# v of two batches by casting transfers, bias rows pair by pair, and a new order of early transfers in an attention and mixer kernel on one Trainium2 core

## The chip, the cores and the metric

The kernel runs on one core of a Trainium2 chip. A core has engines with instruction queues of their own: PE (TensorE, matmuls and transposes), DVE (VectorE), ACT (ScalarE), POOL (GpSimd) and SP (SyncE, which here only issues transfers). Transfers that SP issues are on one hardware queue (q1), those of ACT on another (q10), those of POOL on a software queue (q0); all of them run on the same 16 DMA engines. Only transfers issued by POOL change a type on the way. The metric is the device time of one execution in microseconds, less is better. "The span" is the time from the first to the last instruction in one profiled execution.

## The reference

For 8 batches, 8 heads, 576 positions and a head width of 64, attention with a causal mask and a bias of running sums, and then a mixer:

```python
scores = scale * np.matmul(q, k.transpose(0, 1, 3, 2))
cum = np.cumsum(np.maximum(s, 0.0), axis=-1)
bias = -(cum[:, :, :, None] - cum[:, :, None, :])
scores = np.where(causal, -1000000000.0, scores + np.minimum(bias, 0.0))
attn = softmax(scores)
x = np.matmul(attn, v)              # heads side by side: 8 x 576 x 512
h = x.transpose(0, 2, 1) @ U @ V    # U: 576 x 32, V: 32 x 576
u = x + h.transpose(0, 2, 1)
out = u + np.maximum(u @ w_ch1, 0.0) @ w_ch2   # 512 x 2048, 2048 x 512
```

All inputs and the output are float32. `softmax` stands for the lines of the reference that subtract the maximum, take exp and divide by the sum.

## The kernel before, in words

**Stages.** Batches are taken in groups of two. For a batch, each head has `scores` (L290): matmuls of transposed keys with transposed queries in four PSUM banks, four exps on ACT into a buffer `p`, and one mask by POOL (`affine_select`, L317). `weigh` (L334) multiplies `p` with `v_raw`, whose rows have a 65th column of ones, so that the sums come along; DVE divides into `x_sb`. For a group, `mix` (L449; `mix_first` for batch 0) adds the low-rank part and transposes into `uT`, `layer1` makes `hT` with w1 and ReLU, `layer2` makes the output with w2.

**Bias.** It is part of the matmul: under the 64 rows of a head's keys and queries lie four more (`AUG`), with ones against the running sums, which are split in three bf16 parts. Keys and queries of a pair of heads are one slot of `kT` and `qT`, a ring of 8 slots; slots 0 to 3 are `kA[0]`, `qA[0]` (batch 0) and 4 to 7 `kA[1]`, `qA[1]` (batch 1). `direct_rows` (L239) sends the parts of batches 0 and 1 from `parts` straight into the slots. For batches 2 to 7 `keep_rows` (L246) stores them in DRAM (`aug`) and `bias_rows` (L257) loads four rows of a pair for the keys and four for the queries.

**Keys and queries.** Batches 0 and 1: `load_six` (L158) loads them as bf16 by POOL, PE transposes them (`turn_six`, L265) and DVE or ACT copies them into the slots. Batches 2 to 7: `cast(b)` (L149) is two transfers by POOL from k and q to bf16 in DRAM (`kq`); `turn_kq` (L165) is two transposing transfers by SP from there into a slot. `turn_batch(b)` (L708) issues `turn_kq` for the four pairs of a batch, each followed by the bias rows of the pair before.

**v.** `fetch_v(b, t)` (L184) loads a tile of 128 rows (the last of 64) as float32 by SP, 256 bytes a row and head, into `vf` (batch 1: into the memory of w2, `vf1`). `cast_v` (L190) turns it into bf16 in `v_raw` on POOL or DVE.

**Order.** The schedule is written out by hand, and each engine works in program order. The start (from L560) loads, clears and sums for batch 0. `first_attention` (L626) has the eight heads of batch 0, with `fill` matmuls between that give no result, then its eight weighs among `mix_first`. Batch 1 is `second_scores`, a generator with `second_at_head(h)` (L715) called after each head; `beside(back, ahead, ratio, lead)` (L545) steps two generators in turn by their costs, with `ahead` held back for `lead` units. L756 puts `layer1` of batch 0 beside batch 1's heads, weighs and mix. From L793 on, the two layers of a group stand beside the attention of the next one; `attention` calls `at_head(h)` (L773) after each head, which issues the transposes, casts and v of later batches. The first mask buffers `first_p` are eight, some lent from `x_sb[1]` and `v_flat[1]`.

Of the kernel before, what the change touches and what calls it, by code (L numbers as in the profile page):

```python
# [40 lines left out]
def kernel(  # L41
# [61 lines left out]
    def clear(ap, value=0.0, engine=None):  # L103
# [9 lines left out]
    vf1 = w2[:, :10, :].bitcast(FP32).rearrange(  # L113
        "p (t a) (b d) -> p t (a b) d", a=2, d=D
    )
# [65 lines left out]
    def staged(b):  # L181
        return vf1 if b == 1 else vf0

    def fetch_v(b, t):  # L184
        rows = slice(128 * t, min(128 * t + 128, S))
        nc.sync.dma_start(
            out=staged(b)[v_rows(t), t], in_=v[b, :, rows].rearrange("h p d -> p h d")
        )

    def cast_v(b, t, engine=None):  # L190
        n = v_rows(t)
        (engine or nc.gpsimd).tensor_copy(v_raw[b // 2 % 2][n, 5 * (b % 2) + t, :, :D], staged(b)[n, t])  # L192
# [46 lines left out]
    def direct_rows(b, p0, p1, r, queue=None):  # L239
        to = qA[b][D : D + 1] if r == 0 else kA[b][D + r : D + r + 1]  # L240
        (queue or nc.sync).dma_start(
            out=to[:, p0:p1, : 2 * S].rearrange("r n (j c) -> r n j c", c=CW),
            in_=parts[2 * SEG * p0 : 2 * SEG * p1, r, b, :],
        )
# [335 lines left out]
    )  # L580
    make_identity(nc, identity)
    load_six(0, 0, 2, 4)
# [28 lines left out]
    direct_rows(0, 0, HP - 1, 1)  # L611
    direct_rows(0, 0, HP - 1, 0, nc.scalar)
    next(sums)
    direct_rows(0, 0, HP - 1, 2)
    next(sums)
    direct_rows(0, 0, HP - 1, 3, nc.scalar)
    for t in (4, 0, 1, 2, 3):
        fetch_v(0, t)
    for r in range(AUG):
        direct_rows(0, HP - 1, HP, r)  # L620
    load_UV(0)
    for n in range(HP, RING):
        clear(qT[n][D:KA, : 2 * S], 1.0, nc.gpsimd)
    later = cumulate(2, B, nc.gpsimd)

    def first_attention():  # L626
# [11 lines left out]
        turns = [(2, 0, "f"), (2, 1, "pv"), (3, 0, "pv"), (3, 1, "f")]  # L638
        done = []
        for h in range(H):  # L640
            p = next_p()
            for _ in scores(h // 2, h % 2, p, fills=320 if 1 < h < 6 else 0):
                pass
            if turns:
                hp, which, tag = turns.pop(0)
                turn_six(0, hp, which, tag=tag)
            done.append((0, h, p))
            if h == 0:
                nc.vector.memset(v_raw[0][:, :, :, D : D + 1], 1.0)
                nc.sync.dma_start(  # L650
                    out=kA[1][D : D + 1].rearrange("r n (h s) -> r (n h) s", h=2),
                    in_=ones[:H],
                )
                for r in range(AUG):
                    direct_rows(1, 0, HP, r)
                load_UV(1)
                nc.sync.dma_start(out=kq[:, :, PAIR:].rearrange("i n c -> (i n) c"), in_=zeros)
                nc.sync.dma_start(
                    out=aug[1:4].rearrange("r n s -> n r s"),
                    in_=ones.unsqueeze(1).to_broadcast([BH, 3, S]),  # L660
                )
                for t in (4, 0, 1, 2, 3):
                    fetch_v(1, t)
            if h == 5:
                for t in range(5):
                    fetch_v(2, t)
            if h == 1:
                clear(U_cat[:, :, :], 0.0, nc.gpsimd)
            if h in (2, 3):
                load_six(1, 0, 4 * h - 8, 4 * h - 4)  # L670
                load_six(1, 1, 4 * h - 8, 4 * h - 4)
            if h == 3:
                load_w1(0)
                clear(V_cat[:, :, :], 0.0, nc.gpsimd)
            if h == 4:
                for t in (4, 0, 1, 2, 3):
                    cast_v(0, t, nc.vector)
                nc.vector.memset(v_raw[0][:64, TAIL], 0.0)
                place_UV(0)
            if h == 5:  # L680
                load_w1(1)
        for j in (2, 3):
            load_w1(j)
        nc.gpsimd.memset(v_raw[0][:64, 5 + TAIL], 0.0)
        halves = [mix_first(dt) for dt in (0, 2)]
        for _ in range(2):
            weigh(*done.pop(0))
        turn_six(1, 0, 0, scalar=2, tag="f")
        for _ in range(2):
            weigh(*done.pop(0))  # L690
        turn_six(1, 0, 1, scalar=2, tag="f")
# [3 lines left out]
        next(second_front)  # L695
        next(second_front)
        weigh(*done.pop(0))
        next(halves[0])
        weigh(*done.pop(0))
# [3 lines left out]
        next(second_front)  # L703
        next(second_front)
# [10 lines left out]
    def second_at_head(h):  # L715
        if h == 2:
            cast(2)
        if h == 3:
            place_UV(1)
        if h == 5:  # L720
            for t in (4, 0, 1):
                cast_v(1, t)
            for n in range(2 * HP, 3 * HP):
                turn_kq(n)
        if h == 6:
            for t in (2, 3):
                cast_v(1, t, nc.vector)
            next(later)
        if h >= 6:
            load_w2(2 * h - 12)  # L730
            load_w2(2 * h - 11)
# [5 lines left out]
    def second():  # L737
        yield from second_front
        for head in second_done:
            weigh(*head)  # L740
            yield 0.48
            next(later, None)
        keep_rows(2, B)
        for n in range(2 * HP, 3 * HP):
            bias_rows(n)
# [11 lines left out]
    for t in range(5):  # L757
        fetch_v(3, t)
    turn_batch(3)

    def both_layers(g):
        if g == 0:
            yield from layer2(0, range(4))
            yield from layer1(((576, 864), (864, 1152)))
            yield from layer2(0, range(4, 9))
        else:
            yield from layer1(THIRDS)
            yield from layer2(g, range(9))

    def ahead_of(c):  # L770


        def at_head(h):  # L773
            if h == 0 and 2 < c < B - 1:
                turn_batch(c + 1)
            if h == 4 and c + 2 < B:
# [16 lines left out]
    for g in range(len(GROUPS)):  # L793
# [5 lines left out]
        n_back = 46.8 if g == 0 else 61.4  # L799
        lead = 14.0 if g == 0 else 0.0  # L800
# [31 lines left out]
```

## Time and profile before

| | |
|---|---|
| runs | 391.14, 389.36, 390.70 us; median 390.7 |
| profiled execution | 390.39 us, span 388.7 us |
| mean granted clock of TensorE | 0.996 |
| transfers | 48.56 MB, 117,991 records |
| q0 (POOL) | 13,824 records, 13.63 MB, 22.4% of 16 engines' span |
| q1 (SP) | 103,558 records, 34.27 MB, 44.1% |
| batch 0, head 0: first scores on PE | 11.01 us |
| batch 2, head 0 | 86.62 us |
| batch 3, head 0 | 109.14 us |

How to read it. A line of a time line has the start in us, the duration, the engine, the line of the kernel, the operation, what it writes and reads, how many were merged, and in brackets how long the engine had been idle before and what ended that. "SPq" and "POOLq" rows, and POOL rows with DMA in the name, are instructions that issue a transfer; their duration is that of the issue, the data land later. Tiles have the names of their memory, so p buffers that are lent show as `x_sb` or `v_raw`, and the sums of batches 2 to 7 as `v_raw`. In a table by stretches each row has the stretch, its length, then busy time and count for PE, PEld (loading of weights, beside PE), DVE, ACT, POOL, then the granted clock as a share of full speed, the busy share of the 16 DMA engines (over 1 where records of several queues overlap) and GB/s. The trace also has a record for every piece that a DMA engine moved, with queue, start, duration and size as written.

### The profile page before, as it was taken

Reading aid. Unit: us, or ns where it says so; the run is one execution under the profiler, and the core shown is the slowest. Engines: PE = TensorE matmul, PEld = TensorE weight load, DVE = VectorE, ACT = ScalarE, POOL = GpSimd, SP = SyncE. Lnnn points to the kernel's source line nnn. Section 1 sums busy time; section 2 is a strip of 40 time slices with the busy share of each in tenths; the row PEclk is TensorE's granted clock in tenths of the full one; section 3 lists DMA queues with packets and bytes.
Section 4 is the critical chain, followed back from the end, with each engine's and each line's share of the span. In section 5 each row is a group of like instructions: output and inputs, shape, how many; then the busy total and the mean of one; then the engine's idle time right before and its main releaser. Section 6 shows DMA issues by size and latency. Waiting matters only on the chain.

```text
span 388.7 us, 8287 instructions
## 1 busy us (share of the span) xinstructions
PE 370.3 (95%) x3277; PEld 228.6 (59%) x3300; DVE 142.1 (37%) x308; ACT 209.1 (54%) x488; POOL 105.4 (27%) x173
## 2 busy tenths in 40 slices
PE   7879898989999999999999999999999999999995
PEld 3567675547876546666655456666655455665442
DVE  7867785222224392212143571212143570000221
ACT  5876984109996207898842007898842005773000
POOL 8981695013544301333142001233120000000000
PEclk9989999999999999999999999999999999999999
DMA  7999999999999969999996417800011111000122
GB/s 109 173 210 214 191 196 169 195 155 207 180 192 232 191 132 254 187 179 147 174 185 170 93 74 133 155 2 2 2 49 38 53 69 41 0 2 27 65 71 81
DMA packets 117991, 48.56 MB, mean 125 GB/s; under 512 B 99576, under 2 KB 113088, under 8 KB 117952
## 3 DMA queue, kind: packets, MB, share of 16 engines
q1 hardware_dynamic: 103558, 34.27, 44.1%
q0 software_dynamic: 13824, 13.63, 22.4%
q8 instruction: 26, 0.43, 0.5%
q10 hardware_dynamic: 570, 0.12, 0.2%
q14 instruction: 13, 0.11, 0.1%
HBM read 37.52 MB, written 16.97 MB: 140 GB/s over the span
## 4 chain that ended last, share of the span: by engine, by line
PE 80%; ACT 5%; DVE 5%; DMA 4%; SPq 3%; issue 1%; ACTq 0%; POOL 0%; DVEq 0%
PE ps_f L509 30%; PE ps_f L524 27%; PE ps_s L296 10%; PE ps_pv L346 7%; DMA kT<-parts 2%; SPq L170 2%; ACT pT L302 2%; PE ps_f L451 2%; PE ps_pv L469 2%; PE ps_f L484 2%; DMA qT<-aug_rows 1%; DVE qT L282 1%; DVE x_sb L488 1%; ACT hT L516 1%; DVE v_raw L224 1%
## 5 line engine op out<-in xcount | busy, mean ns | idle before, releaser
L509 PE MATMUL ps_f<-uT,w 128*128 128x384 bf16 (+3 forms) x832 | 157.6, 313 | 0.2 <-ACT hT L516 0.2
L302 ACT ACTIVATE pT<-ps_s 128x448 bf16<-128x448 f32 x232 | 109.1, 520 | 69.3 <-PE ps_s L296 68.0
L524 PE MATMUL ps_f<-w,hT 128*128 128x512 bf16 x554 | 138.7, 379 | 1.3
L516 ACT ACTIVATE hT<-ps_f 128x384 bf16<-128x384 f32 (+2 forms) x208 | 99.4, 479 | 65.9 <-PE ps_f L509 64.5
L509 PEld LDWEIGHTS <-w 128*128 128x128 bf16 x832 | 72.7, 98 | 33.8 <-issue 0.7
L317 POOL TENSOR_SCALAR_AFFINE_SELECT pT<-pT 128x640 bf16<-128x640 bf16 x58 | 43.6, 752 | 168.2 <-ACT pT L302 168.1
L296 PE MATMUL ps_s<-qT,kT 68*128 68x128 bf16 (+9 forms) x576 | 81.4, 240 | 7.4 <-DMA kT<-parts 3.1
L524 PEld LDWEIGHTS <-hT 128*128 128x128 bf16 x576 | 53.2, 98 | 55.0 <-issue 2.2
L296 PEld LDWEIGHTS <-kT 68*128 68x128 bf16 (+1 forms) x576 | 46.6, 97 | 37.0 <-issue 6.9
L533 DVE TENSOR_TENSOR o<-x_sb,ps_f 128x512 f32<-128x512 bf16 x36 | 24.7, 686 | 95.0 <-PE ps_f L524 81.1
L352 DVE RECIPROCAL rec<-ps_pv 128x5 f32<-128x5 f32 x64 | 12.4, 194 | 126.2 <-PE ps_pv L346 126.0
L346 PEld LDWEIGHTS <-pT 128*128 128x128 bf16 x870 | 34.7, 99 | 8.9 <-ACT pT L302 1.5
L346 PE MATMUL ps_pv<-v_raw,pT 128*128 128x65 bf16 x870 | 37.6, 196 | 1.0 <-ACT pT L302 0.7
L358 DVE TENSOR_TENSOR x_sb<-ps_pv,rec 128x320 bf16<-128x320 f32 (+1 forms) x64 | 29.3, 458 | 2.3
L488 DVE TENSOR_TENSOR x_sb<-x_sb,ps_f 128x512 bf16<-128x512 bf16 x32 | 21.2, 685 | 5.7 <-PE ps_f L484 5.6
L192 POOL CAST v_raw<-vf 128x512 bf16<-128x512 f32 (+1 forms) x30 | 17.9, 612 | 0.4
L476 DVE COPY uT<-ps_pv 128x1024 bf16<-128x1024 bf16 (+2 forms) x18 | 11.1, 623 | 2.5 <-PE ps_pv L469 2.4
L469 PEld LDWEIGHTS <-x_sb 128*128 128x128 bf16 x128 | 8.6, 98 | 4.1 <-DVE x_sb L488 0.2
L484 PE MATMUL ps_f<-ux_sb,V_cat 128*128 128x512 bf16 x27 | 10.2, 379 | 0.6 <-DVE o L533 0.4
L469 PE MATMUL ps_pv<-identity,x_sb 128*128 128x128 bf16 x128 | 10.3, 219 | 0.1
L288 PE MATMUL ps_s<-uT 128*128 128x512 bf16 (+1 forms) x22 | 8.1, 445 | 1.8 <-DVE uT L105 1.6
L451 PE MATMUL ps_f<-x_sb,U_cat 128*128 128x512 bf16 x31 | 8.7, 379 | 0.7 <-DVE x_sb L363 0.7
(104 smaller groups left out, 160.2 us busy)
## 6 DMA issues: line engine op xcount, KB each, us to landing
out_dram<-o SPq DMA_DIRECT2D x32, 256.0 KB
vf<-in_v_dram SPq DMA_DIRECT2D x28, 256.0 KB
w<-in_moe_w_ch_dram POOLq DMA_DIRECT2D x8, 512.0 KB, 9.9
kq_rows<-in_k_dram POOLq DMA_DIRECT2D x6, 576.0 KB, 6.5
kq_rows<-in_q_dram POOLq DMA_DIRECT2D x6, 576.0 KB, 9.6
w<-in_v_dram SPq DMA_DIRECT2D x4, 256.0 KB
out_dram<-o SPq DMA_DIRECT2D x8, 128.0 KB
vf<-in_v_dram SPq DMA_DIRECT2D x7, 128.0 KB
```

Source lines behind the costliest of these rows:

```text
L296: nc.tensor.matmul(ps[:, col : col + w], lhsT=kt_[:rows, c + kc : c + kc + 128], rhs=qt_[:rows, c + qc : c + qc + w], start=True, stop=True,)
L302: nc.scalar.activation(p[:, at : at + w], ps[:, :w], EXP, scale=scale)
L317: nc.gpsimd.affine_select(out=diagonal, in_=diagonal, compare_op=ALU.is_ge, fill=0.0, base=0, pattern=[[0, 5], [1, 128]], channel_multipli ...
L346: nc.tensor.matmul(pv3[:, it, :], lhsT=p[:, at : at + 128], rhs=vr[:, 5 * bi + j, h, :], start=(j == 0), stop=(j == it),)
L358: nc.vector.tensor_mul(x[:, 5 * bi : 5 * bi + n, h * D : h * D + D], pv3[:, :n, :D], rec[:, :n].unsqueeze(2).to_broadcast([128, n, D]),)
L469: nc.tensor.transpose(pb[:, d, m, :], x[:, t, 128 * d : 128 * d + 128], identity)
L484: nc.tensor.matmul(hp_, lhsT=V_cat[:, t, :], rhs=ux_sb, start=True, stop=True,)
L488: nc.vector.tensor_add(x[:, t, :], x[:, t, :], hp_)
L509: nc.tensor.matmul(f1[:, :cw], lhsT=w1[:, kt, 128 * nf : 128 * nf + 128], rhs=uT[:, kt, c0:c1], start=(kt == 0), stop=(kt == 3),)
L516: nc.scalar.activation(hT[:, nf, c0:c1], f1[:, :cw], RELU)
L524: nc.tensor.matmul(f2, lhsT=hT[:, kt, 128 * t : 128 * t + 128], rhs=w2[:, kt, :], start=(kt == 0), stop=(kt == 15 and not more),)
L533: nc.vector.tensor_add(o, x_sb[g % 2][:, t, :], f2)
```

## The change

- v of batches 0 and 1 comes by `load_v`, a transfer by POOL that writes bf16 in place into `v_raw`; the float32 stage in w2's memory, ten fetches by SP and ten casts go.
- Batch 0's bias rows go pair by pair: pair 0 first, then pairs 1 and 2, then pair 3, on SP. `direct_rows` writes the same bytes with heads and pieces as one dimension.
- Clears move from POOL to DVE; the ones under batch 1's queries come by three transfers by SP from `ones` instead of four clears.
- `load_six` of batch 1 is issued before the heads of batch 0, behind `load_v(0)`. Two turns of batch 1 go into heads 6 and 7 of batch 0, with all copies on DVE.
- Heads 0 to 2 of batch 0 are weighed after the scores of heads 5 to 7; batch 1's first ten steps go between the other weighs (four steps before).
- w2 is loaded at heads 1 to 4 of batch 1 (6 and 7 before), ahead of the cast of batch 2, which moves from head 2 to 5. The sums of batches 2 to 7 start at head 3 and are stored at head 7; behind them SP fetches v of batch 2 and turns batch 2 with its rows pair by pair.
- The cast of batch 3 (the "third cast"), its v and its transposes move from before batch 2's attention to behind its head 1.
- The first tile of `layer2` of group 0 moves into the stage beside batch 1, and the ratios follow.

The diff, cut to its core:

```diff
@@ the start
-    make_identity(nc, identity)
     load_six(0, 0, 2, 4)
+    make_identity(nc, identity)
     load_six(0, 1, 2, 4)
+    nc.vector.memset(v_raw[0][:, :, :, D : D + 1], 1.0)
...
-    for p in first_p:
-        nc.gpsimd.memset(p[:, PAD:D4], 1.0)
-    clear(ones, 1.0, nc.gpsimd)
-    clear(zeros, 0.0, nc.gpsimd)
+    for t in (4, 0, 1, 2, 3):
+        load_v(0, t)
+    for hs in ((0, 4), (4, 8)):
+        for i in range(2):
+            load_six(1, i, *hs)
...
-    direct_rows(0, 0, HP - 1, 1)
-    direct_rows(0, 0, HP - 1, 0, nc.scalar)
+    direct_rows(0, 0, 1, 1)
+    direct_rows(0, 0, 1, 0, nc.scalar)
...
-    for t in (4, 0, 1, 2, 3):
-        fetch_v(0, t)
-    for r in range(AUG):
-        direct_rows(0, HP - 1, HP, r)
+    for p0, p1 in ((1, HP - 1), (HP - 1, HP)):
+        for r in (1, 2, 0, 3):
+            direct_rows(0, p0, p1, r)
     load_UV(0)
-    for n in range(HP, RING):
-        clear(qT[n][D:KA, : 2 * S], 1.0, nc.gpsimd)
@@ new
+    def load_v(b, t):
+        rows = slice(128 * t, min(128 * t + 128, S))
+        nc.gpsimd.dma_start(
+            out=v_raw[0][v_rows(t), 5 * b + t, :, :D],
+            in_=v[b, :, rows].rearrange("h p d -> p h d"),
+        )
@@ first_attention, before the heads
+        clear(ones, 1.0)
+        clear(zeros, 0.0)
+        for p in first_p:
+            nc.vector.memset(p[:, PAD:D4], 1.0)
+        for i in (0, 1):
+            nc.vector.memset(v_raw[0][:64, TAIL + 5 * i], 0.0)
...
+        turns = [
+            (0, 2, 0, "f"), (0, 2, 1, "pv"), (0, 3, 0, "pv"), (0, 3, 1, "f"),
+            None, None, (1, 0, 0, "f"), (1, 0, 1, "f"),
+        ]
@@ in the heads
+            for _ in scores(h // 2, h % 2, p, fills=320 if 1 < h < 5 else 0):
...
+            if h >= 5:
+                weigh(*done.pop(0))
+            if h == 4:
                 load_w1(0)
+                clear(U_cat[:, :, :])
+                clear(V_cat[:, :, :])
+        weigh(*done.pop(0))
+        place_UV(0)
+        for j in (1, 2, 3):
             load_w1(j)
@@ second_at_head
+        if h == 0:
+            for t in (4, 0, 1, 2, 3):
+                load_v(1, t)
         if h == 2:
+            place_UV(1)
+        if 1 <= h <= 4:
+            load_w2(h - 1)
+        if 3 <= h:
+            next(later)
+        if h == 5:
             cast(2)
+        if h == 7:
+            keep_rows(2, B)
+            for t in range(5):
+                fetch_v(2, t)
+            turn_batch(2)
@@ second
-        nc.gpsimd.tensor_copy(warm[:1, :1], qT[2 * HP + HP - 1 - RING][:1, :1])
-        cast(3)
-    beside(layer1(PARTS, by_block=True), second(), 15.2 / 14.9, 0.0)
-    for t in range(5):
-        fetch_v(3, t)
-    turn_batch(3)
+    def first_layer():
+        yield from layer1(PARTS, by_block=True)
+        yield from layer2(0, range(1))
+    beside(first_layer(), second(), 15.2 / 18.3, 0.0)
@@ at_head of the later batches
+            if h == 1 and c == 2:
+                nc.gpsimd.tensor_copy(warm[:1, :1], qT[2 * HP + HP - 1 - RING][:1, :1])
+                cast(3)
+                for t in range(5):
+                    fetch_v(3, t)
+                turn_batch(3)
@@ the last loop
-        n_back = 46.8 if g == 0 else 61.4
-        lead = 14.0 if g == 0 else 0.0
+        n_back = 43.4 if g == 0 else 61.4
+        lead = 10.0 if g == 0 else 0.0
```

More of the change, by code (lines that the diff above doesn't have):

```diff
@@ L680, in first_attention @@
-            if h == 5:
-                load_w1(1)
-        for j in (2, 3):
+            if turns[h]:
+                b, hp, which, tag = turns[h]
+                turn_six(b, hp, which, tag=tag)
+            if h >= 5:
+                weigh(*done.pop(0))
+            if h == 4:
+                load_w1(0)
+                clear(U_cat[:, :, :])
[3 more added lines that the diff above has]
+        for j in (1, 2, 3):
             load_w1(j)
-        nc.gpsimd.memset(v_raw[0][:64, 5 + TAIL], 0.0)
@@ L685, in first_attention, with more @@
         halves = [mix_first(dt) for dt in (0, 2)]
[L686 to L691, printed above, removed]
+        def more(n):
+            for _ in range(n):
+                next(second_front)
+        more(2)
+        weigh(*done.pop(0))
+        more(2)
+        weigh(*done.pop(0))
+        more(2)
+        next(halves[0])
         weigh(*done.pop(0))
@@ L694, in first_attention @@
         weigh(*done.pop(0))
[L695 to L699, printed above, removed]
+        more(2)
         for _ in halves[0]:
@@ L702, in first_attention @@
         next(halves[1])
-        next(second_front)
-        next(second_front)
+        more(2)
         for _ in halves[1]:
```

88 lines of the change are left out of this document (22 added, 66 removed).

## The prediction

> **What bounds the kernel now.** I read the busy shares first, then the table by stretches, then the time lines of PE, SP and POOL around each wait of PE.
>
> ```profile
> PE 370.3 (95%) x3277; PEld 228.6 (59%) x3300; DVE 142.1 (37%) x308; ACT 209.1 (54%) x488; POOL 105.4 (27%) x173
> 0.00:11.00 11.00, 7.16 (x40) 3.05 (x41) 8.29 (x23) 5.46 (x8) 9.40 (x30) 1.00 0.82 115
> 11.00:19.50 8.50, 7.91 (x83) 5.51 (x84) 6.63 (x10) 8.10 (x21) 7.94 (x13) 1.00 0.96 175
> 19.50:24.50 5.00, 2.75 (x22) 1.52 (x20) 3.43 (x6) 3.67 (x10) 3.96 (x8) 0.92 1.32 210
> 24.50:35.00 10.50, 10.04 (x177) 8.75 (x175) 7.03 (x21) 6.93 (x14) 5.35 (x8) 0.88 1.26 216
> 35.00:55.00 20.00, 17.84 (x217) 13.55 (x217) 16.10 (x28) 17.82 (x48) 12.70 (x20) 1.00 1.12 197
> 200.00:240.00 40.00, 39.66 (x289) 21.61 (x291) 18.60 (x35) 9.32 (x21) 5.63 (x9) 1.00 0.53 125
> ```
>
> PE carries the end: from 95 us on it is over 98% busy until the tail. What an edit can win lies before that: about 11 us in which PE waits, and what fills (no result) and a low clock take. The column before last is the DMA share: in the first 95 us it is near or above 1, so there the transfers are the second bound. The waits of PE, with what ended them, and batch 3, which has none:
>
> ```profile
> 11.01 0.74 PE L296 MATMUL ps_s<-qT,kT 128*128 128x64 bf16 x7 [1.29 <-DMA kT<-parts]
> 21.96 0.74 PE L296 MATMUL ps_s<-qT,kT 128*128 128x64 bf16 x7 [1.76 <-DMA kT<-parts]
> 86.62 0.36 PE L296 MATMUL ps_s<-qT,kT 68*128 68x64 bf16 x4 [1.00 <-DMA qT<-aug_rows]
> 109.14 0.36 PE L296 MATMUL ps_s<-qT,kT 68*128 68x64 bf16 x4
> ```
>
> Heads 0 and 6 of batch 0 and head 0 of batch 2 wait for bias rows. Why rows and transposes can be late is on SP and POOL:
>
> ```profile
> 80.30 0.83 POOL L151 DMA_DIRECT2D kq_rows<-in_k_dram  x1
> 97.43 1.40 SPq L170 DMA_TRANSPOSE qT<-kq_rows  x1
> 99.18 0.74 POOL L151 DMA_DIRECT2D kq_rows<-in_k_dram  x1
> 102.06 6.16 SPq L170 DMA_TRANSPOSE qT<-kq_rows  x1
> 108.28 0.47 SPq L261 DMA_DIRECT2D kT<-aug_rows  x1
> ```
>
> A transpose takes 1.4 us alone and 6.16 us under the cast of batch 4 (issued 99.18). The DMA records of the trace say why: while both queues have work, POOL's (q0) and SP's (q1) alternate one record at a time, 281 against 282 at 46 to 48 us and 824 against 830 at 124 to 130, one pair per engine in about 0.115 us. Alone, q1 moves a 256-byte record per engine in about 16.5 ns. A transpose and a v fetch are 72 and 64 such records per engine, a cast of k or q 32.
>
> **The change part by part**, against the profiled execution (span 388.7, time 390.39; the runs' median, 390.7, is 0.3 higher and within their spread).
>
> Start. Pair 0's bias rows go alone: 18 pieces instead of 54. Row 3 was issued by ACT at 6.29 and landed at 10.76; its records began 2.1 to 2.4 us after the issue and trickled to 10.4, alternating with the six loads. With a third of them I put the landing at 9.2. The queries are copied at 8.7 and the second transposes are limited by their load (8.85 now), so head 0 starts at 9.4 instead of 11.0: **-1.6** (bounds 0 and -2.3, by the copies). The identity moved behind one load costs the first transposes 0.2, hidden behind DVE's sums, which run to 5.8 and free the copy. Pairs 1 to 3 follow on SP at 0.75 each and land near 12 and 15, ahead of heads 2 and 6: the 1.3 us that ACT lost before head 6 go (**-1.3**).
>
> Weights early. Three weighs at 0.48 and two turns at 0.25 leave the PE-bound stretch after 24.7 for heads 5 to 7, where ACT is the bound (1.6 us a head): **-1.9**.
>
> v by casting transfers. Removed: five DVE casts (3.2 us), five more of batch 1 (3.7 on POOL and DVE), ten SP fetches. Added: ten POOL issues; those of 192, 384 and 512 rows took 0.64, 0.68 and 0.76, so about 0.95 for 1024, 4.6 us per batch, with four loads of batch 1 (2.7) behind them. The clears that leave POOL (3.3 us) make room, and head 0's mask runs at about 17 instead of 13.1, which only the first weigh reads. The DVE clears (1.7) fall into its 1.5 us gap before 12.56; DVE is then full until 19 and head 6 waits 0.4 for it. The price that the trace lacks is a cast of 256 bytes. Lower bound: the plain 256-byte record, 18 ns. The line through the cast records (79, 96 and 106 ns for 1536, 2048 and 2304 bytes read) gives 34. Upper: 34 + 13 = 47, since a plain 128-byte record doubles from 13 to 26 where it is crowded. A cast of 2048 adds 12 ns to the plain 84, so 18 + 12 = **30 ns**, which I take: it starts from the record of the same size. 288 of them: 8.6 us per batch behind the six loads (11.3), so v(0) lands at 20.4 and the first k of batch 1 at 22.3. Weigh 0 wants v at 18.2, and PE is about 0.5 ahead of ACT there: **+1.7** (0 to 6.5, by the bounds); the turns at heads 6 and 7 wait **+0.7**. Together -1.6 - 1.3 - 1.9 + 1.7 + 0.7 = **-2.4** by the time layer 1 begins.
>
> Batch 1. Its heads start sooner, but DVE has more: the later sums (0.69 + 6 x 0.43 = 3.3 us) sit at head 3 instead of 6, among turns of 1.6 a head. I take 0 (-1 to +1.5). On q0 the rest follows without a gap: batch 1's q and k from 19.9 (4 x 1.85, by the spacing of their records), w1 (4 x 3.1), v(1) 8.6, w2 (4 x 3.1) to 61, the cast of batch 2 (2 x 3.5) to 68, and 2 us for what SP alternates in: 70. Layer 2 needs w2 near 67; were it late, PE would stand that long.
>
> Batch 2. SP fetches v(2), then has four transposes (1.35 each) and pair 0's rows: landed near 79. Before, keep_rows and rows came last. PE gets there at 86.6 - 1.0 - 2.4 = **83.2**, so the 1.0 wait goes: **-1.0**. Layer 2's first tile ahead of it is only moved, and `lead` falls with it.
>
> Batch 3. Here I expect the loss. The cast of batch 3 was issued at 80.30, 6.3 us ahead of batch 2; now it waits behind head 1's mask, 4.7 us after batch 2's start (88.19 + 2.9 - 86.62): 87.9, its records from 89.4 (1.5 after issue, as at 81.84 now). POOL's wait for the last transpose (84.8) is over by then; if not, the masks queue behind it. SP, done with batch 2's rows near 84 (8 x 1.35 + 4 x 0.65 after 70.5), sends four outputs (1.8 as now) and v(3), whose records start near 89. The cast of batch 4 follows at head 4 (12.6 after batch 2's start, as now), so q0 holds 2 x 64 = 128 records without a gap. q1 must move v(3), 288, and four transposes, 288, before pair 0's rows. Alternating: 128 x 0.115 = 14.7, to 104.1; the other 448 at 16.5 ns, 7.4, to 111.5; rows 0.5: **112.0**. PE arrives at 83.2 + 22.5 (109.14 - 86.62) + 0.2 (the new ratio) = 105.9. Stall: **+6.1**, and +0.2 for the ratio. The next pairs need 3.5 us each and heads use 5.5, so this happens once.
>
> Clock. After the 1.76 us wait at 20 the granted clock was 0.74 and 0.58 in two stretches of 2.5 us: 1.7 us lost. The 6 us wait I give the same, less what ACT's pace hides: **+1.5** (0 to 1.7); the early dip may recur behind the wait for v and I leave it in.
>
> Sum: -2.4 - 1.0 + 6.1 + 0.2 + 1.5 = +4.4, so 390.4 + 4.4 = **394.8**. v at 25 to 36 ns instead of 30 moves 576 records by -2.9 to +3.5: 392 to 398 is the likeliest case's own range.
>
> A rule against this. The Trainium skill (DMA: Bandwidth & Descriptors, Queues, rings and completion order) says that an engine goes round its queues a packet at a time, typically 9 to 17 descriptors. By it SP's 72 records would wait some 4 to 8 turns and no transpose would starve, which is the first rival's case; the counts of one to one and the 6.16 us speak against it here.
>
> **Rivals.** (1) Batch 3's data come in time: SP's records get through the casts. Then from the cast's landing (about 14 after batch 2's start) three transposes at 1.4 and rows end near 19, under 22.7, and the result is 390.4 - 3.4 + 0.2 = 387.2. For: batch 3 has 7 us in hand now. Against: the alternation. (2) A cheap v, 20 ns: 5.8 us per batch, no wait for v, PE at batch 2 at 81 and q0 done 5 us sooner, v(3) half through before the cast; batch 3 then waits about 3: 390.4 - 5.8 + 0.2 + 3 + 1 = 389. (3) A dear v: above about 45 ns v(0) lands at 24.8 and the wait at weigh 0 is 6 instead of 1.7; both batches together push the cast of batch 2 by 8.6 to near 79, the last transpose past 93 and, through POOL's wait, the records of the cast of batch 3 from 89.4 to 95.5: batch 3 starts near 118, and the time is 390.4 + 9 + 1.5 = 401.
>
> **How the numbers follow.** Forecast 0.53, rival 1 0.17, rival 2 0.15, rival 3 0.13, nothing of this 0.02. Predicted 394.8. The range 387 to 398.5 takes in rivals 1 and 2 and leaves out the dear v and tails; the likeliest alone has 392 to 398. About 0.5% (2 us) is what a measurement can tell: slower 0.60 (most of the forecast, rival 3), same 0.20 (rival 2, the forecast's low end), faster 0.20 (rival 1, some of 2).
>
> **What would show it.** Right: head 0 at 9 to 10; a wait of PE near 18 to 20 on v_raw from in_v; v's cast records near 30 ns; no wait at batch 2; one of 4 to 8 us at batch 3's first head on kT or qT, with two transposes of 5 us or more just before, then a dip of the clock. Wrong: batch 3 without a wait (rival 1), or PE waiting for w2, or for v of batch 1.

## The result, and the profile after

The changed kernel took 395.76 us (median of four runs, 394.49 to 397.32), the kernel before 390.92 (389.36 to 393.07) beside it: ratio 1.0125, 95% interval 1.0088 to 1.0162, slower by 4.8 us. Where a median of the kernel before stands below, it is over all its runs on that chip; the ratios leave disturbed runs out.

The profiled execution of the changed kernel is the longest of the four: 397.32, span 395.6, against 388.7 before. First the busy shares, then the table by stretches:

```profile
PE 371.8 (94%) x3298; PEld 229.6 (58%) x3298; DVE 141.9 (36%) x318; ACT 206.2 (52%) x484; POOL 106.5 (27%) x163
```

```profile
11.00:19.50 8.50, 7.48 (x79) 5.10 (x80) 8.16 (x21) 7.76 (x20) 8.45 (x13) 1.00 2.14 146
19.50:24.50 5.00, 4.50 (x79) 3.37 (x77) 3.66 (x8) 4.87 (x14) 3.20 (x5) 1.00 1.35 206
24.50:35.00 10.50, 7.96 (x130) 6.80 (x127) 8.31 (x20) 3.84 (x10) 8.58 (x13) 0.84 1.18 202
75.00:95.00 20.00, 20.00 (x186) 12.87 (x184) 4.13 (x9) 10.27 (x28) 4.56 (x7) 1.00 0.77 174
95.00:115.00 20.00, 12.51 (x164) 9.94 (x161) 3.43 (x10) 11.35 (x31) 7.25 (x11) 0.84 1.18 184
115.00:135.00 20.00, 20.00 (x228) 13.93 (x226) 6.15 (x19) 15.31 (x37) 8.32 (x12) 0.90 1.03 188
```

PE's total is nearly the same. It is fuller than before from 19.5 to 24.5 and from 75 to 95, and emptier from 24.5 to 35 (7.96, it was 10.04). From 95 to 115 it is missing 7.5 us, and the clock stays down into the next stretch. The time line of PE has the waits:

```profile
11.06 0.74 PE L297 MATMUL ps_s<-qT,kT 128*128 128x64 bf16 x7 [1.02 <-DMA kT<-parts]
20.48 0.62 PE L347 MATMUL ps_pv<-v_raw,pT 128*128 128x65 bf16 x15
26.85 0.91 PE L297 MATMUL ps_s<-qT,kT 68*128 68x64 bf16 x6 [1.27 <-DMA w<-in_moe_U_dram]
84.16 0.55 PE L297 MATMUL ps_s<-qT,kT 68*128 68x64 bf16 x6
113.75 0.53 PE L297 MATMUL ps_s<-qT,kT 68*128 68x64 bf16 x4 [7.40 <-DMA qT<-aug_rows]
```

Head 0 still starts at 11; the wait ahead of head 6 is gone (head 6 at 20.94, it was 21.96); the first weigh (20.48) does not wait for v; batch 1's head 0 has a new wait (the bracket names a load of U, which these matmuls do not read; experiments 9 and 10 show what ended it); batch 2 starts without one, 2.46 earlier than before; batch 3 waits 7.40 for its bias rows. How they came to be late is on SP, with the casts of POOL (88.68 is the third, 96.50 the fourth) between:

```profile
86.54 4.24 SPq L187 DMA_DIRECT2D vf<-in_v_dram  x5
96.42 2.57 SPq L167 DMA_TRANSPOSE kT<-kq_rows  x1
100.06 3.09 SPq L167 DMA_TRANSPOSE qT<-kq_rows  x1
103.25 5.27 SPq L167 DMA_TRANSPOSE kT<-kq_rows  x1
108.61 2.01 SPq L167 DMA_TRANSPOSE qT<-kq_rows  x1
110.72 0.43 SPq L262 DMA_DIRECT2D kT<-aug_rows  x1
...
111.61 1.25 SPq L167 DMA_TRANSPOSE kT<-kq_rows  x1
```

```profile
88.68 0.77 POOL L148 DMA_DIRECT2D kq_rows<-in_k_dram  x1
...
96.50 0.73 POOL L148 DMA_DIRECT2D kq_rows<-in_k_dram  x1
```

The third cast is issued 8.4 us later than before (80.30); SP then stands until 96.42 for the cast's keys; the four transposes run beside the casts and take 2 to 5 us each; the next one, after the casts, takes 1.25.

**Where the time went.** One instruction serves as a mark far behind, first in the kernel before, then in the changed one:

```profile
177.75 0.39 PE L346 MATMUL ps_pv<-v_raw,pT 128*128 128x65 bf16 x7 [0.27 <-ACT pT L302]
```

```profile
184.93 0.39 PE L347 MATMUL ps_pv<-v_raw,pT 128*128 128x65 bf16 x7 [0.27 <-ACT pT L303]
```

Behind it both executions need the same (211.0 and 210.7). From batch 2's first scores to the mark the kernel before needs 91.13. The same difference, for all kernels of this study (of each the profiled execution; waits of PE over 0.45 us in between; what is then left):

| kernel | batch 2 head 0 | mark | between, less 91.1 | waits | left |
|---|---|---|---|---|---|
| before | 86.62 | 177.75 | 0.0 | none | 0.0 |
| changed | 84.16 | 184.93 | 9.7 | 7.40 | 2.3 |
| early_third | 83.10 | 180.58 | 6.4 | 4.17 | 2.2 |
| fourth_later | 83.16 | 183.53 | 9.3 | 2.14, 2.44 | 4.7 |
| third_only | 84.22 | 184.55 | 9.2 | 6.49 | 2.7 |
| v_only | 87.83 | 178.96 | 0.0 | none | 0.0 |
| v_only_early_ones | 87.36 | 178.48 | 0.0 | none | 0.0 |
| rows_whole | 83.43 | 182.48 | 8.0 | 6.73 | 1.2 |
| pair_first | 82.53 | 179.51 | 5.9 | 2.88 | 3.0 |
| pair_first_fourth7 | 83.39 | 184.44 | 10.0 | 1.17, 5.99 | 2.8 |
| mended | 83.17 | 185.54 | 11.3 | 0.49, 2.66, 4.21 | 3.9 |
| mended_uv_later | 84.13 | 186.00 | 10.8 | 0.48, 8.34 | 1.9 |
| fourth_in_batch3 | 82.53 | 179.98 | 6.4 | 5.18 | 1.2 |
| fourth_in_batch3_fifth7 | 82.33 | 173.43 | 0.0 | none | 0.0 |

All four kernels without such a wait need 91.1, whatever stands ahead. So the changed kernel wins 2.5 by batch 2 and loses 7.4 to one wait and 2.3 behind it: +7.2 at the mark, +6.9 in the span.

What is left goes with the clock. In half-microsecond stretches of the changed kernel the granted clock falls to 0.50 at 108.7, 2.4 us after PE ran dry (106.35), and is 1.00 again at 119.0, 5.2 us after PE resumed (113.75): 5.2 at half speed is 2.6, and 2.3 is missing. The same holds in all ten kernels with a wait: behind it PE worked 3.4 to 10.0 us at half clock, and what is left is 0.67 to 0.98 of half of that. The Trainium skill (TensorE: Matmul & The Clock Gate, Part 1: The HAM clock gate) has the clock halved after an idle window of about 3.4 us and the first 3.4 us or so of new work at half speed, varying from run to run since the window runs free. The two states agree. The delays differ: PE had been idle for 2.4 us when the clock fell, and half speed lasted 5.2 us into the new work.

### The profile page after: what moved, and what is told of

It is laid out like the page before. It is cut to its first block, busy times and chain, and to the rows that moved or that the text cites. A ratio compares the mean times of both kernels' runs of the same rounds, so it can differ in the third digit from the quotient of the medians.

```text
span 395.6 us, 8299 instructions
## 1 busy us (share of the span) xinstructions
PE 371.8 (94%) x3298; PEld 229.6 (58%) x3298; DVE 141.9 (36%) x318; ACT 206.2 (52%) x484; POOL 106.5 (27%) x163
## 4 chain that ended last, share of the span: by engine, by line
PE 85%; DMA 5%; DVE 4%; SPq 2%; ACT 1%; issue 1%; ACTq 0%; DVEq 0%
PE ps_f L510 31%; PE ps_f L525 30%; PE ps_s L297 10%; PE ps_pv L347 7%; PE ps_f L452 2%; PE ps_pv L470 2%; DMA w<-in_moe_V_dram 2%; DMA kT<-parts 2%; PE ps_f L485 1%; DMA w<-in_moe_U_dram 1%; SPq L167 1%; DVE x_sb L489 1%; DVE qT L283 1%; ACT pT L303 1%; DMA qT<-aug_rows 1%
## 5 line engine op out<-in xcount | busy, mean ns | idle before, releaser
L525 PE MATMUL ps_f<-w,hT 128*128 128x512 bf16 x576 | 143.0, 379 | 0.3
L297 PE MATMUL ps_s<-qT,kT 68*128 68x128 bf16 (+9 forms) x576 | 83.1, 244 | 12.4 <-DMA qT<-aug_rows 7.4
L353 DVE RECIPROCAL rec<-ps_pv 128x5 f32<-128x5 f32 x64 | 12.5, 195 | 136.1 <-PE ps_pv L347 136.1
L289 PE MATMUL ps_s<-uT 128*128 128x512 bf16 (+1 forms) x20 | 7.2, 446 | 1.6 <-DVE uT L105 1.6
```

What stands on the lines that cost most here:

```text
L297: nc.tensor.matmul(ps[:, col : col + w], lhsT=kt_[:rows, c + kc : c + kc + 128], rhs=qt_[:rows, c + qc : c + qc + w], start=True, stop=True,)
L525: nc.tensor.matmul(f2, lhsT=hT[:, kt, 128 * t : 128 * t + 128], rhs=w2[:, kt, :], start=(kt == 0), stop=(kt == 15 and not more),)
```

## The experiments

The theory: the earlier start is worth its 3 us or so, and the loss is one mechanism, SP's transfers alternating record by record with a cast, which makes batch 3's transposes late; a clock dip follows. Rivals: v by casting is itself dear; the gain is lost anyway, whatever batch 3 does.

**1. The third cast alone** (third_only: the kernel before, with only the third cast, v(3) and the turns of batch 3 moved).

```diff
@@ second(), behind mix(0)
-        cast(3)
@@ behind the first layer
-    for t in range(5):
-        fetch_v(3, t)
-    turn_batch(3)
@@ at_head
+            if h == 1 and c == 2:
+                cast(3)
+                for t in range(5):
+                    fetch_v(3, t)
+                turn_batch(3)
```

> The kernel before with one part of the change: the third cast, v of batch 3 and its transposes are issued behind head 1 of batch 2. Theory: the same loss in the old kernel, a wait of 4 to 8 us at batch 3's first head and a clock dip of 1.5 to 2, so 396 to 400. Rival A or B: within 2 us of the kernel before, 389 to 393.

Measured: 397.44 (396.85 to 402.67), ratio 1.020 (1.0127 to 1.0273) to the kernel before at 390.91 on that chip. PE's line at batch 3's head 0:

```profile
113.43 0.53 PE L296 MATMUL ps_s<-qT,kT 68*128 68x64 bf16 x4 [6.49 <-DMA qT<-aug_rows]
```

This one move, without any other part of the change, makes the wait and a loss no smaller than that of the whole change. It also starts batch 2 earlier than before (84.22 against 86.62), as batch 2's last bias rows, issued behind that cast before, have nothing beside them now (read from the traces, not tried by itself).

**2. The third cast back in its place** (early_third: the changed kernel with only that part undone).

```diff
@@ second(), behind mix(0)
+        cast(3)
@@ behind the first layer
+    for t in range(5):
+        fetch_v(3, t)
+    turn_batch(3)
@@ at_head
-            if h == 1 and c == 2:
-                cast(3)
-                for t in range(5):
-                    fetch_v(3, t)
-                turn_batch(3)
```

> The changed kernel with one part undone: the third cast, v of batch 3 and its transposes are issued where the kernel before had them, behind batch 1's mix. Theory (the loss is batch 3's wait, made by the late cast): no wait of PE at batch 3's first head, batch 3 at about 106.4 instead of 113.75, no dip of the clock behind it, and 395.8 - 7.4 - 2 = about 386.5, faster than the kernel before by 4. Rival A (the cast's lateness is not it, batch 3 waits for SP or for v): a wait of over 4 us stays, over 391. Rival B (v on POOL's queue costs the time all along): over 393.

Measured: 392.87 (392.26 to 393.38), ratio 1.0044 (1.0018 to 1.0070). Better than the changed kernel by 3, and the theory's 386.5 is missed. SP and PE say why:

```profile
79.94 11.19 SPq L187 DMA_DIRECT2D vf<-in_v_dram  x5
...
97.36 6.18 SPq L167 DMA_TRANSPOSE qT<-kq_rows  x1
```

```profile
109.45 0.53 PE L297 MATMUL ps_s<-qT,kT 68*128 68x64 bf16 x4 [4.17 <-DMA qT<-aug_rows]
```

v(3)'s reads now go out right behind the third cast and share with it (11.19 us for five issues that take 3.9 to 4.2 with nothing beside them), so the turns start at 91; the fourth cast, issued at 95.44 since batch 2 is earlier, catches the fourth one (6.18). Before, pair 0's rows left at 98.92, 0.26 us ahead of the fourth cast at 99.18: they were clear of it by no more than that.

**3. The fourth cast later** (fourth_later: the changed kernel with the fourth cast at head 7 of batch 2 instead of 4).

```diff
-            if h == 4 and c + 2 < B:
+            if h == (7 if c == 2 else 4) and c + 2 < B:
```

> The changed kernel, but the fourth cast is issued at head 7 of batch 2 instead of head 4; the third cast stays late. Theory (the late transposes starve beside the fourth cast, record by record): the four transposes before pair 0's rows take 1.3 to 2 us each, the wait at batch 3 falls from 7.4 to under 2, and the time to 387 to 389. Rival C (lateness alone: cast, landing and four transposes in a row do not fit into seven heads): the wait stays at 4 us or more, 392 or more.

Measured: 394.46 (394.05 to 395.9), ratio 1.0100 (1.0060 to 1.0141). PE's waits:

```profile
107.49 0.53 PE L297 MATMUL ps_s<-qT,kT 68*128 68x64 bf16 x4 [2.14 <-DMA qT<-aug_rows]
...
117.31 0.36 PE L297 MATMUL ps_s<-qT,kT 68*128 68x64 bf16 x4 [2.44 <-DMA qT<-aug_rows]
```

Without the fourth cast beside them pair 0's turns take 1.2 to 2.1 us and the first wait falls from 7.40 to 2.14: most of the wait was the fourth cast's doing. The 2.14 that stay are the late start (the third cast is issued at 87.68, its keys are there for SP at 95.28, four transposes follow) and the rows, issued at 104.27 with the fourth cast beside them again; the two were not told apart. The time of 387 to 389 is missed, for the cast, now issued at 103.54, catches a turn of pair 1 (106.99, 5.55 us). A second wait appears, with a second dip of the clock.

**4 and 5. v by casting alone** (v_only: the kernel before with `load_v` for batches 0 and 1 in place of fetches, stage and ten casts; v_only_early_ones: the same with the column of ones in `v_raw` written before the transfers).

```diff
-    for t in (4, 0, 1, 2, 3):
-        fetch_v(0, t)
+    for t in (4, 0, 1, 2, 3):
+        load_v(0, t)                 # ahead of the clears of first_p, on POOL
...
-                for t in (4, 0, 1, 2, 3):
-                    cast_v(0, t, nc.vector)
...
+        for t in (4, 0, 1, 2, 3):
+            load_v(1, t)             # behind load_w1(3)
@@ v_only_early_ones, besides
+    nc.vector.memset(v_raw[0][:, :, :, D : D + 1], 1.0)   # behind the clear of qT[0]
-                nc.vector.memset(v_raw[0][:, :, :, D : D + 1], 1.0)   # at head 0
```

> The kernel before with one part of the change: v of batches 0 and 1 by casting transfers into place, issued by POOL behind the start's clears and behind the last load of w1; the float32 stages and ten casts of these batches go. Theory (the casting transfers are cheap, records of 32 ns that overlap): no wait for v at the first weighs, SP reaches v of batch 2 some 14 us sooner, batch 2's wait of 1.0 us goes, 388.5 to 390.5. Rival B: slower than the kernel before by 2 or more.

> The kernel before with v of batches 0 and 1 by casting transfers, as in the earlier run of that part alone, but with the column of ones in v written before the transfers instead of at head 0 (there VectorE waited 4.55 us for the transfers, and TensorE 3.05 us for the turns behind it). Leaves nothing out. Theory (casting v in place takes ten copies off VectorE and GpSimd and costs the queues little, so it is worth the stall it removes ahead of head 6): 3 us less than that run, 388 to 389.5. Rival (the transfers' records cost the rest of the start what the copies gave): 390.5 to 392.

Measured: 391.84 (390.77 to 394.76), ratio 1.0035 (1.0001 to 1.0069), and 392.29 (390.64 to 394.6), ratio 1.0016 (0.9974 to 1.0057) to 391.53 on its chip. In the first, DVE's clear of the ones stood 4.55 us behind the transfers into the same rows, and PE 3.05 behind DVE; in the second that wait is gone, and the time is the same. Its PE time line:

```profile
87.36 0.36 PE L297 MATMUL ps_s<-qT,kT 68*128 68x64 bf16 x4 [1.94 <-DMA qT<-aug_rows]
```

What PE had won (scores of batch 1 at 38.06 that stood at 39.07) it gives back at v of batch 1 (a wait of 0.70 at 52.39) and at batch 2's head 0, whose rows land no sooner, as its turns were not moved. So v by casting is neither dear nor, by itself, worth anything that these runs can tell: a rival falls, and with it my 388.5 to 390.5 for the first and 388 to 389.5 for the second.

**6. The rows of batch 0 as before** (rows_whole: the changed kernel with three pairs' rows at once).

```diff
-    direct_rows(0, 0, 1, 1)
+    direct_rows(0, 0, HP - 1, 1)     # likewise rows 0, 2 and 3
```

> The changed kernel with batch 0's bias rows in three pairs at once and the fourth pair behind, as the kernel before has them, in place of pair by pair. By the prediction's step (pair 0's small rows land earlier and head 0 starts 1.6 us earlier) this would be 1.6 us slower than the changed kernel, 397.4, with head 0 at about 12.5. By what the two traces show (head 0 waits for the rows until 11.06 against 11.0, because the first record of a row's transfer starts 2.4 us after its issue however many pieces it has): within 0.7 us of the changed kernel, head 0 between 10.8 and 11.5.

Measured: 395.81 (395.13 to 396.67), ratio 1.0123 (1.0020 to 1.0226); head 0 at 11.11, not 12.5. Pair by pair or not makes no difference to head 0. The interval of the time is too wide to tell 1.6 us by itself.

**7 and 8. Pair 0 ahead of v(3)** (pair_first: early_third with SP's order pair 0, v(3), pairs 1 to 3; pair_first_fourth7: and the fourth cast at head 7).

```diff
-    for t in range(5):
-        fetch_v(3, t)
-    turn_batch(3)
+    turn_batch(3, lambda: [fetch_v(3, t) for t in range(5)])
@@ turn_batch(b, behind_first=None)
             turn_kq(n)
-            if n > HP * b:
+            if n == HP * b and behind_first:
+                bias_rows(n)
+                behind_first()
+            elif n > HP * b + (1 if behind_first else 0):
                 bias_rows(n - 1)
```

> The changed kernel with the third cast back between the first layer's halves, and of batch 3 only pair 0 (two turns and their two bias rows) issued ahead of the five reads of v; the fourth cast stays at head 4 of batch 2. Theory (the changed kernel pays for the wait at batch 3's head 0 and the slower clock behind it, nothing else): the third cast runs with no plain read beside it and lands 7 to 9 us after its issue at 79.4, pair 0's rows land by 93, 12 us ahead of head 0 of batch 3 at about 105; no wait there, 386 to 388 us, faster than both kernels. Rival 1 (the wait only moves to a later pair, as when the fourth cast alone was moved): pair 1's turns run beside the fourth cast, end near 108, and a wait of 2 to 4 us appears at batch 3's head 2: 390 to 392. Rival 2 (what the other parts won at the start is lost again by the chain of ScalarE in any case): no wait, and still within 0.5% of the kernel before.

> The same, and the fourth cast issued at head 7 of batch 2 instead of head 4, so that pairs 1 to 3 are turned between the two casts. Theory (turns take 1.3 us each when no cast runs beside them and up to 6 us when one does): the six turns of pairs 1 to 3 take 1.2 to 2 us each and no wait stands anywhere in batch 3: 386 to 388. Rival 1 (the fourth cast, 8 us later, makes batch 4's turns late instead): a wait of 3 us or more at batch 4's head 0, 389 to 392. Rival 2 as for the kernel before it: no wait, and 389 or more.

Measured: 392.42 (391.83 to 395.69), ratio 1.0038 (0.9999 to 1.0077), and 396.61 (396.06 to 396.81), ratio 1.0134 (1.0050 to 1.0219). PE's waits, first kernel, then second:

```profile
112.03 0.53 PE L297 MATMUL ps_s<-qT,kT 68*128 68x64 bf16 x4 [2.88 <-DMA qT<-aug_rows]
```

```profile
111.16 0.36 PE L297 MATMUL ps_s<-qT,kT 68*128 68x64 bf16 x4 [1.17 <-DMA qT<-aug_rows]
...
134.01 1.00 PE L347 MATMUL ps_pv<-v_raw,pT 128*128 128x65 bf16 x15 [5.99 <-POOL pT L318]
```

Batch 3's head 0 waits in neither. In the first, the fourth cast catches pair 1 instead (5.83 and 4.00 us for its turns), as rival 1 had it. In the second, pairs 1 and 2 take 1.3 to 2.4, pair 3 has the fourth cast (103.76) beside it (5.19 for its second turn), and the reads of v(4), issued at 119.39, take 11.90; POOL's next masks stand behind the casts of that v. Both theory values are missed, by a wait that moves each time.

**9 and 10. The fourth cast between** (mended: pair_first with each pair's rows straight behind its turns and the fourth cast at head 6; mended_uv_later: besides, U and V of batch 0 loaded behind batch 1's direct rows).

```diff
-            if h == 4 and c + 2 < B:
+            if h == (6 if c == 2 else 4) and c + 2 < B:
@@ mended_uv_later
-    load_UV(0)
@@ first_attention
             direct_rows(1, 0, HP, r)
+        load_UV(0)
         load_UV(1)
```

> The changed kernel with the third cast back between the first layer's halves, pair 0 of batch 3 ahead of the reads of v, each pair's bias rows straight behind its turns, and the fourth cast at head 6 of batch 2 (between head 4, where pair 1 was starved, and head 7, where the reads of v for batch 4 were). Leaves nothing out. Theory (what is lost against the earlier start is only waits for turns and reads that run beside a cast, and the slower clock behind such a wait): pair 1 is turned by 102, ahead of the fourth cast at about 101, its rows land by 107, ahead of its need at 109; v of batch 4 is read from 117 on, behind that cast; no wait over 0.5 us from 75 us on, head 0 of batch 3 at about 106, clock 1.00 from 95 us on: span 385 to 386.5, time 386.5 to 388, ratio 0.988 to 0.993. Rival 1 (some pair is late wherever the fourth cast stands, since SyncE's row of turns, rows and reads has no room left): a wait of 1 to 3 us at a later pair or for v of batch 4, 389 to 392. Rival 2 (the clock falls without such a wait): no wait, clock under 0.95 somewhere in 95 to 135, 389 or more.

> The same, and the loads of U and V of the first projection issued behind batch 1's direct rows instead of ahead of the rows of ones, which brings batch 1's rows some 2 us forward on SyncE. Theory (batch 1's head 0 waits 1.27 us for rows that SyncE issues from 18.0 to 21.9 and that land near 26): the wait at about 26.5 goes, and U and V, issued at 20 to 23, land ahead of GpSimd's placing at 24.9: 0.8 to 1.5 us less than the kernel without this edit. Rival (the rows' records share the queues with the casts of batch 1's q and k and of the first weights, and land as late as before): no difference over 0.3 us, and the wait stands.

Measured: 397.47 (396.9 to 398.87), ratio 1.0146 (1.0101 to 1.0191), and 397.64 (397.07 to 398.38), ratio 1.0141 (1.0088 to 1.0194). Lines of SP and of POOL in mended:

```profile
120.73 11.64 SPq L187 DMA_DIRECT2D vf<-in_v_dram  x5
```

```profile
131.62 0.61 POOL L193 CAST v_raw<-vf 128x512 bf16<-128x512 f32 x1 [11.13 <-DMA vf<-in_v_dram]
```

Rival 1 again in kind, though the waits and the time are larger than it had (389 to 392). It names the next collision: the rows of pair 3 (a wait of 2.66 at 123.68) and the reads of v(4) run beside the *fifth* cast (117.91, head 4 of batch 3).

The U and V move changes nothing in the time: batch 1's head 0 waits 1.31 us at 26.54 where it waited 1.53 at 27.19. The bracket of these lines names a load of U, because such loads share semaphores with the rows. The landing events in the traces tell more. In mended the last of batch 1's rows lands at 27.14 and ends the wait. In mended_uv_later it lands at 24.30, so the move did bring the rows forward; but the queries of the pair are still being copied by DVE, and PE's wait for that copy ends with it, at 26.1 (the matmul follows 0.4 us later, as in the changed kernel):

```profile
24.48 1.61 DVE L283 COPY qT<-ps_f 64x576 bf16<-64x576 bf16 x2
```

```profile
26.54 0.91 PE L297 MATMUL ps_s<-qT,kT 68*128 68x64 bf16 x6 [1.31 <-DMA w<-in_moe_U_dram]
```

In the changed kernel row and copy are there together (26.46 and 26.43). So the rival, that the rows land as late as before, falls, and the theory fails for another reason: the copy was next in line.

**11 and 12. Both casts moved** (fourth_in_batch3: pair_first with the fourth cast at head 0 of batch 3, behind all turns of pairs 1 and 2; fourth_in_batch3_fifth7: and the fifth at head 7 of batch 3, behind the casts of v(4)).

```diff
+            if h == 0 and c == 3:
+                cast(4)
             if h == 0 and 2 < c < B - 1:
                 turn_batch(c + 1)
-            if h == 4 and c + 2 < B:
+            if h == 4 and c != 2 and c + 2 < B:
@@ fourth_in_batch3_fifth7
+            if h == (7 if c == 3 else 4) and c != 2 and c + 2 < B:
```

> The kernel with pair 0 of batch 3 ahead of the reads of v (third cast between the first layer's halves), and the fourth cast at head 0 of batch 3, behind the turns of pairs 1 and 2; the fifth stays at head 4 of batch 3. Leaves nothing out. Theory (each wait so far stood where turns or reads of v ran beside a cast; SyncE has room for them only between two casts): pairs 1 and 2 are turned from 97 to 105 with no cast beside them, pair 3 by 109, v of batch 4 is read from 111 to about 118, a little of it beside the fourth cast; no wait over 0.5 us in batch 3, masks not held, clock 1.00: 386.5 to 388.5, ratio 0.987 to 0.993. Rival 1 (the collision moves once more, to the reads of v of batch 4 beside the fourth or the fifth cast): GpSimd waits for v of batch 4 for 3 us or more near 120 and its masks hold TensorE near 130, 391 to 395. Rival 2 (no wait, but the kernel is no faster than before, as the clock or later stages take it back): 389.5 to 392.

> The same with the fifth cast at head 7 of batch 3, behind the casts of v of batch 4, instead of head 4. Theory: the reads of v of batch 4 have only the fourth cast's end beside them and land by 119; batch 4's turns run beside the fifth cast, and nothing needs them before 150: 386.5 to 388.5 whichever way the kernel before it comes out. Rival 1: the reads of v are late in this one too (the fourth cast alone is enough), 391 to 395. Rival 2 as above, 389.5 to 392.

Measured: 392.51 (392.18 to 393.58), ratio 1.0076 (1.0047 to 1.0106), and **386.33** (385.4 to 387.09), ratio **0.9910** (0.9876 to 0.9944). The first still has the reads of v(4) at 112.08 beside both casts (13.23 us) and a wait of 5.18 behind POOL. The last has no wait of PE over 0.45 us from 75 us to the mark. The stretch that had the wait, and SP around batch 3:

```profile
95.00:115.00 20.00, 19.72 (x254) 15.23 (x252) 5.48 (x17) 18.30 (x50) 9.51 (x14) 1.00 1.13 187
```

```profile
102.36 1.30 SPq L167 DMA_TRANSPOSE qT<-kq_rows  x1
...
111.88 10.79 SPq L187 DMA_DIRECT2D vf<-in_v_dram  x5
```

Batch 3's query turns take 1.2 to 1.5; reads beside the fourth cast still take 10.79 for five, but end early enough; the starved turn at 128.31 (4.96) is batch 4's, which nothing needs yet. The clock is 1.00 there and in the stretch behind. The change's other parts are thus worth 0.9% once the casts stand elsewhere, and the theory, whose time six kernels had missed by a wait at the next reader, is borne out by the one in which no such reader is left. Against the changed kernel's ratio of 1.0125 this is 2.1% less (on two chips, each beside the kernel before).

## Why the prediction was right, point by point

The forecast was 394.8, the range 387 to 398.5, and the likeliest case the one that came: the cause of the loss is the one forecast. That the figure is within 1 us of the median is in part luck, as several terms were off and their errors offset each other.

- **Start, -1.6: wrong, 0.** The step was that 18 pieces land sooner than 54. Row 3, the last of pair 0, was issued by ACT at 6.38 and its records ran from 8.96 to 10.26: the first comes 2.6 us behind the issue, although only 18 pieces follow, the last lands at 10.82 (10.76 before), and head 0 starts at 11.06. rows_whole has the same with 54 (10.86 and 11.11). I had both numbers (2.1 to 2.4 us to the first record) and still let the number of pieces decide.
- **The stall ahead of head 6, -1.3: -1.0** (21.96 to 20.94).
- **v by casting, +1.7 and +0.7: wrong, 0 and 0.** The record takes 32 ns (I took 30), but I laid the records end to end. They overlap: the DMA share of 11 to 19.5 us is 2.14 (0.96 before), and at the busiest 1,766 (v of batch 0) and 2,159 (batch 1) of them start in 2 us on 16 engines, one in 15 to 18 ns each, as fast as a plain record of 256 bytes. Over the whole of a v it is one in 19 to 22. v(0)'s records end at 17.6, and weigh 0 runs at 20.48 without a wait. Weighs and turns in heads 5 to 7 (-1.9) came as stated: PE is busy 4.50 of 5 us from 19.5 to 24.5 where it was 2.75.
- **Batch 1, 0 (-1 to +1.5): inside, at its dear end.** New waits of 1.27 (the last row, and the copy of the queries on DVE) and 1.06 (a copy of `ux` queued on DVE behind a turn's copies); in some executions, this one among them, the clock falls to 0.50 from 26.8 to 30.2, in others with the same start (pair_first, mended) it stays 1.00. Batch 2's head 0 lies between 83.4 and 84.2 in the four traces with that dip and between 82.3 and 83.2 in the six others with nearly this start; I had 83.2. The sum of the early terms held by luck, because two errors of 1.6 and 2.4 were of opposite sign.
- **Batch 2, -1.0: right**, no wait. w2 was never late.
- **Batch 3, +6.1: right in kind, 7.40.** Predicted against measured: cast issued 87.9, 88.68; PE there at 105.9, 106.35; the last transpose's records through at 111.5, 112.2; rows landed at 112.0, 113.61. The mis-sized term is "rows 0.5": from the last transpose's records to the first matmul it is 1.6 us. The agreement at 111.5 is partly luck too. The two casts' records ran for 18.5 us (90.98 to 109.50), where the sum had 14.7 (89.4 to 104.1); in return 2,807 of v(3)'s 4,608 records were through before the third cast's first.
- **The alternation** that I took from the trace of before was there again (280 records of q0 against 281 of q1 between 96 and 98 us). Equal counts alone would also fit queues that take turns by packets of equal length. The starts decide it: from 124 to 130 us of the kernel before, those of SP's records recur every 114 ns, as those of POOL's do (correlation with themselves 0.88 at that distance, no more than 0.1 from 14 to 22 ns); SP's alone, from 88 to 90 us of the changed kernel, recur every 14 ns (0.84). The rule of the Trainium skill (DMA: Bandwidth & Descriptors, Queues, rings and completion order) that I weighed, turns of a packet of typically 9 to 17 descriptors, is not what these records show. My reading that it would spare a transpose was also wrong: 4 to 8 turns of 9 to 17 cast records at 0.106 us would be, as an estimate, 4 to 14 us. Beside a cast a transpose took up to 4 to 6 us, between casts 1.2 to 2.4.
- **"This happens once": right here, not in general.** fourth_later, pair_first and the kernels after them showed the next pair, then v(4), each late in turn. The step overlooked that moving one cast frees one reader and catches another.
- **Clock, +1.5: 2.3** by the mark. Half speed lasted 5.2 us behind the wait; I had taken the loss over from a wait of 1.76.
- **Rival 1 (387.2: data in time)** is what fourth_in_batch3_fifth7 makes true by hand: 386.33. The casts were moved away; no record got through one. **Rival 2 (a cheap v)** had the right price for v, with no wait for it, but gave batch 3 a wait of 3, and the early time it promised was not there; v_only shows 0 from it alone. **Rival 3** is out.

The profile sums to +6.9 and the medians to +4.8; the profiled execution is 1.6 above the median. The dip of the clock at 26.8 (3.4 us at half speed, at most 1.7) may be the reason, but that is not shown: the other executions have no trace, and one with the same mean clock (0.983) took 395.87.

One reading of the profile before was too broad: PE is not over 98% busy everywhere from 95 us to the tail; from 135 to 150 it is 95.8%.

What stays open: why the last of batch 1's rows lands at 26.46 although SP issued it at 21.18; that it is the traffic of the casts beside it was argued from the records, and no run without those casts was made. How early batch 1's head 0 could start with both the rows and DVE's copy sooner was not tried. That the clock's dip at 26.8 comes and goes with the same code was seen, not explained.

## What to carry to other kernels

In these runs a transfer's time was set by what else was in flight when its records ran. So list, for every cast or other large transfer, the readers that run beside it and which of them somebody needs soon, and place it where only patient readers stand. When work is pulled forward by a few microseconds, look at what the old schedule cleared by less than that (here 0.26 us between the rows and the fourth cast). When one fix moves a wait to the next reader, keep the mechanism and follow the chain to its end before giving up the change. When the profile names the end of a wait, check that the instruction needs what is named; here a load that nobody read stood for a row and a copy. Compare two kernels between two marks that both have, not by the whole span: a stage that needs 91.1 us in every kernel without a wait tells what each wait and the clock behind it cost.

## What the runs showed of the hardware that was not expected

- Casting records of 256 bytes last 32 ns, but at the busiest an engine starts one every 15 to 18 ns; the DMA share of 2.14 is the sign. A cast of rows of 2,304 bytes read (106 ns) beside plain records does hold the others to one for one, a pair every 114 ns.
- A row of 18 pieces and one of 54 took the same time to land (4.4 to 4.6 us from their issue); some 2.4 us or more of it pass before the first record. The bias rows of batch 3's first pair took 3.0 us from issue to use, since they ran behind a transpose's records.
- The clock fell to 0.50 2.4 us after PE ran dry and came back 5.2 us after it resumed. The cost is not proportional to the wait: one of 4.17 cost 2.2 behind it, one of 7.40 cost 2.3, one of 6.73 cost 1.2. In the clock records of all these traces every fall ahead of the tail lasts 3.41, 6.83 or 10.24 us.
